# A third pass over token pairs in scaled float16 parts, with its second product in seven block products too

## The chip, the cores and the metric

The kernel runs on one core of a Trainium2 chip. The metric is device time in microseconds for one execution. A core has a matrix engine (TensorE, PE in the profile; its weight loads are listed as PEld), a vector engine (DVE), a scalar engine (ACT), GpSimd (POOL) and a queue that issues DMAs (SP). Matmuls read SBUF and write PSUM.

## The reference

Attention over 4 batches, 8 heads, 768 positions of 64, with a local window and block summaries, gives x, 3072 tokens of 512. Then a mixture of four experts works on x, with all experts on every token:

```python
def _moe_ref(x, domain_probs, w1, w2):            # x 3072 x 512, w1 4 x 512 x 1024, w2 4 x 1024 x 512
    p = domain_probs / (domain_probs.sum(-1, keepdims=True) + 1e-09)
    for e in range(E):
        h = np.maximum(x @ w1[e], 0.0)
        out += p[:, e:e + 1] * (h @ w2[e])
    ...

def reference(...):
    attn_out = _attn_ref(...)                     # softmax over a window of +-16 and 24 block summaries
    x = attn_out.transpose(0, 2, 1, 3).reshape(B * S, H * D)
    return _moe_ref(x, ...)
```

All data are float32.

## The kernel before

**Precision.** A float32 operand is split into a high part in fp32r (a rounded form of float32 that TensorE takes in one pass) and a low part, what the high part leaves. A product is three matmuls: high x high, high x low, low x high.

**Tokens and passes.** The 3072 tokens are eight blocks of 384 (`TB`). `plan` lists the passes of the experts over them: block 0 with experts 0 and 1, block 1 with 1 and 0, both with 2 and 3, and then `PAIRS`: pair 1 (blocks 2 and 3) with experts 3, 2, 1, 0, pair 2 (blocks 4, 5) with 0, 1, 2, 3 and pair 3 (blocks 6, 7) with 3, 2, 1, 0. Attention for later blocks runs between the matmuls of earlier passes, in 64 pieces (`load_piece`, `stage_a`, `scores`, `probs`, `transposed`, `values`, `to_x`); `advance` spreads their steps over the passes so that the last piece ends within pair 2's pass. Pair 3's pass has only the experts.

**A pair pass.** `pair_units` does one expert on one pair. The first product, x @ w1, uses seven block products in place of eight: the 2 x 2 blocks are two halves of the 512 rows of w1 and two blocks of 128 columns on one side, two token blocks on the other. For each of four groups i (two blocks of 128 columns of w1), the seven entries of `SEVEN` are six matmuls of 384 columns each, into four PSUM banks a, b, c, d: ACT copies a to b after entry 0 and d to SBUF (`five`) after entry 1, DVE makes c = b + five after entry 2 and d = b + five after entry 4. `to_h` then takes each finished bank: ACT writes relu as the high part, DVE the low part, straight from PSUM. The second product, h @ w2, is plain: `mm2` makes for each of the pair's six tiles of 128 tokens 24 matmuls of 512 columns (8 chunks, three matmuls each), and DVE adds the result, times the token's mixing weight, to `acc`; after the fourth expert the tile goes out by a DMA.

**Operands.** `x_operands` makes the seven sums of x for a pair, each split; `w1_operands` the seven sums of w1 for one group, `split_weights` the parts of w2. The first time (pair 1 for the sums of w1) raw weights are loaded, split by ACT, DVE and POOL, and the split parts are also stored to device memory (`stored`); later passes load the stored parts, 28 of 256 KB for w1 and 8 of 512 KB for w2 per expert. `fetch` runs one group ahead of the products, and `with_fetch` loads two groups during the second product.

**Order.** After the first tokens' part, order on each engine is set by the tile framework: it simulates a timeline with its own costs and issues by priority, which is the order of the code; `high_priority(offset=RUSH)` moves the PSUM copies, sums and relus ahead. Engines then run their queues in that order. Buffers come by tag with a fixed number each: x 14 (`NX`), w1 14 (`NW1`), w2 8, wr (raw weights) 4, hs 2, hh and hl 16 each, acc 6. Every engine call passes through one helper line (75), so the profile names groups by their tiles: `po` is the second product's PSUM, `pha` to `phd` the banks of a pair's first product, `psc` and `px` attention's, `w1s` and `w` parts of weights, `hh` and `hl` parts of h.

## Time and profile before

| | |
|---|---|
| median of 3 runs | 1188.52 us (1187.16 to 1191.98) |
| the profiled execution, time | 1190.1 us |
| its span, first to last instruction | 1188.3 us |
| mean granted TensorE clock | 0.994 |
| instructions | 19862 |
| DMA, q1 | 248.34 MB, 69.5% of 16 engines' span |
| HBM read / written | 174.22 / 57.15 MB |

Pair 1's pass runs from about 384 to 663 us after the span's start, pair 2's to 935, pair 3's to the end. In the views, a line of a group has the shapes, the count, the busy time in us, the mean length of one in ns, and the idle time before with what ended it. A line of the timeline or of the chain has the start and the time in us; with "x3", three instructions of that kind were merged, and the time reaches from the first one's start to the last one's end. An instruction's length reaches from its start to its written result; the next one on the engine may start before that.

### The profile page before, as it was taken

The page shows a single profiled execution, that of the slowest core. Times are in us where ns is not written, and L with a number is a line of the kernel's source. Part 1 is how long each engine was busy: PE and PEld are TensorE (multiplying, and loading weights), DVE is VectorE, ACT ScalarE, POOL GpSimd, SP SyncE. Part 2 cuts the span into 40 slices and gives each one's busy share as a digit, 9 for nine tenths or more (in the row PEclk, how much of TensorE's full clock was granted, in tenths as well). Part 3 has the DMA queues.
Part 4 walks back from the last instruction along what each step waited for, and adds up shares of the span by engine and source line. Part 5 has one row for each costly group of instructions (what it writes and reads, how often), then busy time and mean ns, then how long its engine had stood idle before and what let it go on. Part 6 is the DMA issues. An engine that isn't in the chain of part 4 may idle for free.

```text
span 1188.3 us, 19862 instructions
## 1 busy us (share of the span) xinstructions
PE 1155.9 (97%) x6740; PEld 1018.8 (86%) x6740; DVE 640.2 (54%) x1567; ACT 544.3 (46%) x1594; POOL 473.2 (40%) x586
## 2 busy tenths in 40 slices
PE   9898899999998999999999999999999999999998
PEld 7788778888977989888898988989898998989896
DVE  6668585554797756648587543535345322323131
ACT  5577567664665746547375443535333220202020
POOL 2388686855696746546384222222203000000000
PEclk9989999999999999999999999999999999999999
DMA  6699869975986879879973758769471556556421
GB/s 238 220 283 262 241 173 270 264 198 148 319 239 193 271 236 263 245 247 289 297 240 109 211 167 268 223 195 305 115 229 42 160 176 194 179 181 201 159 98 54
DMA packets 202709, 249.60 MB, mean 210 GB/s; under 512 B 83056, under 2 KB 118896, under 8 KB 202608
## 3 DMA queue, kind: packets, MB, share of 16 engines
q1 hardware_dynamic: 202608, 248.34, 69.5%
q8 instruction: 53, 0.87, 0.3%
q14 instruction: 48, 0.39, 0.1%
HBM read 174.22 MB, written 57.15 MB: 195 GB/s over the span
## 4 chain that ended last, share of the span: by engine, by line
PE 67%; DVE 5%; DMA 2%; POOL 1%; ACT 1%; issue 1%; SPq 0%; DVEq 0%; POOLq 0%; ACTq 0%
PE po L75 37%; PE phb L75 11%; PE pha L75 7%; PE phc L75 4%; PE phd L75 4%; PE psc L75 2%; PE px L75 2%; POOL wr L75 1%; DVE xr L75 1%; DVE w1s L75 1%; DMA wr<-in_w2L 1%; PE ph L75 1%; DVE xl_t L75 1%; DVE ms L75 0%; DVE hl L75 0%
## 5 line engine op out<-in xcount | busy, mean ns | idle before, releaser
L75 PE MATMUL po<-w,hh 128*128 128x512 f32 x1536 | 482.0, 395 | 1.8 <-DVE hl L75 1.8
L75 PEld LDWEIGHTS po<-w,hh 128*128 128x128 f32 x1536 | 284.8, 189 | 63.6 <-DVE hl L75 2.3
L75 PE MATMUL po<-w,hl 128*128 128x512 f32 x768 | 303.2, 397 | 0.2 <-DVE hl L75 0.2
L75 PEld LDWEIGHTS po<-w,hl 128*128 128x128 f32 x768 | 144.7, 188 | 31.9 <-DVE hl L75 0.6
L75 POOL TENSOR_TENSOR ks<-kr,ks 128x304 fp32r<-128x304 f32 x112 | 102.1, 919 | 93.0 <-ACT ks L75 82.5
L75 PE MATMUL phb<-xh_t,w1s 128*128 128x384 f32 x384 | 114.8, 339 | 1.7 <-DVE phc L75 0.8
L75 DVE CUSTOM_DVE_ANT_0 ms<-psc,c_sb 96x152 f32<-96x152 f32 x256 | 69.0, 306 | 85.1 <-PE psc L75 82.2
L75 ACT ACTIVATE ms<-ms,nb 96x152 f32<-96x152 f32 x256 | 104.3, 415 | 19.5 <-DVE nb L75 18.6
L75 PE MATMUL pha<-xh,w 128*128 128x384 f32 x384 | 110.6, 335 | 0.0
L75 DVE SCALAR_TENSOR_TENSOR acc<-po,pw,acc 128x512 f32<-128x512 f32 x72 | 52.2, 747 | 103.9 <-PE po L75 103.9
L75 POOL TENSOR_TENSOR qv<-qv,v 128x256 f32<-128x256 f32 x56 | 42.1, 753 | 161.3 <-ACT v L75 140.0
L75 PE MATMUL ph<-xh,wh 128*128 128x384 f32 x256 | 87.7, 349 | 12.8 <-ACT wh L75 5.3
L75 PE MATMUL ph<-xh,wl 128*128 128x384 f32 x256 | 87.0, 341 | 0.4 <-POOL wl L75 0.3
L75 PE MATMUL ph<-xl,wh 128*128 128x384 f32 x256 | 86.9, 340 | 0.0
L75 ACT CAST v<-qv 128x256 bf16<-128x256 f32 x112 | 44.7, 401 | 87.5 <-PE px L75 73.4
L75 ACT CAST aw<-ms 96x512 f16<-96x512 f32 x112 | 53.4, 524 | 68.2 <-issue 49.1
L75 POOL TENSOR_TENSOR wl<-wr,wh 128x512 fp32r<-128x512 f32 x44 | 60.8, 1386 | 53.2 <-ACT wh L75 50.2
L75 DVE TENSOR_TENSOR aw<-ms,aw 96x512 f16<-96x512 f32 x112 | 71.5, 671 | 16.7 <-ACT aw L75 16.6
L75 PEld LDWEIGHTS phb<-xh_t,w1s 128*128 128x128 f32 x384 | 70.8, 188 | 4.1 <-DVE phc L75 1.7
L75 PEld LDWEIGHTS pha<-xh,w 128*128 128x128 f32 x384 | 70.5, 188 | 0.4
L75 ACT CAST ks<-kr 128x304 fp32r<-128x304 f32 x112 | 48.2, 444 | 40.3 <-PE psc L75 38.0
L75 PE MATMUL phb<-xl_t,w1s 128*128 128x384 f32 x192 | 64.3, 335 | 0.0
(123 smaller groups left out, 2190.2 us busy)
## 6 DMA issues: line engine op xcount, KB each, us to landing
w<-wd SPq DMA_DIRECT2D x80, 512.0 KB, 4.4
w1s<-wds SPq DMA_DIRECT2D x112, 256.0 KB, 3.5
w<-wd SPq DMA_DIRECT2D x84, 256.0 KB, 3.4
wr<-in_w1L SPq DMA_DIRECT2D x76, 256.0 KB, 4.3
qv<-in_qvL SPq DMA_DIRECT2D x56, 320.0 KB, 3.9
wd<-w SPq DMA_DIRECT2D x32, 512.0 KB, 4.0
wds<-w1s SPq DMA_DIRECT2D x64, 256.0 KB, 2.4
kr<-in_kD SPq DMA_DIRECT2D x56, 256.0 KB, 3.7
```

The source lines that it names most:

```text
L75: ins = getattr(self.engine, name)(*a, **kw)
```

## The change

Pair 3's pass is rewritten; passes before it gain what it needs.

- **Scaling.** `SCALED` is pair 3. Maxima of |v| of the last batch (in `setup_v`), of |w1| and of |w2| for each expert (`scan`, called from `w1_operands` on the raw halves and from `pair_units` after entries 4 and 5 on w2's high part, each chunk once, so in pair 1's pass) give powers of two (`scales`) that bring operands near a fixed size; `over_partitions` takes a maximum over the 128 partitions by writing it to device memory and reading it back to all of them. x is multiplied by its scale in `x_operands`, weights as they are split, and `mixed` puts the inverse scales into the mixing weights.
- **float16.** High and low parts of x, w1, h and w2 in pair 3's pass are float16, in place of fp32r.
- **`seven_units`** takes the place of `pair_units` for pair 3. The first product has the same seven entries and six matmuls of 384 columns an entry. ACT now writes relu of each bank as float32 to SBUF, sums of h are made there (four DVE sums a group), and the seven operands of h are split by ACT copies and low parts (three on POOL, four on DVE). The second product uses the same seven entries: for each of three token tiles of the two blocks, seven entries of 12 matmuls with 256 columns, in banks a to d; `add_up` adds a finished bank to 256 columns of `acc`.
- **Weights** of pair 3's pass are not stored parts: `jobs_of` yields, an expert ahead, loads of raw weights and `make_group`, which splits one group of w1 or w2 (ACT casts with the scale, DVE low parts, POOL sums). A step of it is issued after each entry of the second product; those of the pass's first expert during pair 2's last second product. w1's groups take the tag w1; w2's take, for every other expert, the w2 tag or buffers that attention used (`ROOMS`).
- `fetch` covers pairs 1 and 2 only.

```diff
+    SCALED = NTB // 2 - 1
...
+    def over_partitions(m, k, name):
+        room = dram.tile([P, k], F32, name=f"{name}d")
+        SP.dma_start(room, m)
+        every = sb.tile([P, P, k], F32, name=f"{name}e", tag="hs", bufs=2)
+        flat = room.rearrange("p k -> (p k)").rearrange("(o n) -> o n", o=1)
+        SP.dma_start(every.rearrange("p q k -> p (q k)"), flat.broadcast_to([P, P * k]))
+        V.tensor_reduce(m, every.rearrange("p q k -> p k q"), axis=AX.X, op=ALU.max)
...
         def part(ib):
             ...
+            if pr == SCALED:
+                V.tensor_scalar(raw, raw, x_scale[pr][0], None, op0=ALU.mult)
...
+    def scan(e, which, fc, part):
+        ...
+        V.tensor_reduce(
+            t[:, which, fc : fc + 1], part, axis=AX.X, op=ALU.max, apply_absolute_value=True
+        )
+        if len(seen) == 2 * FC:
+            ...
+            over_partitions(m, 2, f"w{e}")
+            s, inv = scales(m, 2, f"w{e}")
...
+        scan(e, 0, 2 * pr, r1)          # in w1_operands, raw halves
+        scan(e, 0, 2 * pr + 1, r2)
...
+    def make_group(which, e, i):
+        s = w_scale[e][which]
+        r1, r2 = raws.pop((which, e, i))
+        ...
+        def parts(names, t, raw):
+            hi, lo = ...
+            A.activation(hi, raw, AF.Copy, scale=s)
+            V.scalar_tensor_tensor(lo, raw, s, hi, op0=ALU.mult, op1=ALU.subtract)
+            ...
+        if which == 0:
+            parts(("11", "12"), a, r1)
+            parts(("22",), d, r22)
+            PL.tensor_tensor(r22, r21, r22, op=ALU.add)
+            PL.tensor_tensor(r21, r11, r21, op=ALU.subtract)
+            parts(("s3", "s1"), b, r2)
+            PL.tensor_tensor(r11, r22, r11, op=ALU.subtract)
+            PL.tensor_tensor(r12, r12, r11, op=ALU.subtract)
+            parts(("s2", "s4"), c, r1)
+        else:
+            ...
+    def jobs_of(e):
+        steps = [(which, e, i) for which in range(2) for i in range(FC // 2)]
+        yield raw_group(*steps[0])
+        for here, after in zip(steps, steps[1:] + [None]):
+            if after:
+                yield raw_group(*after)
+            yield make_group(*here)
...
-    for pr, es in PAIRS:
+    for pr, es in PAIRS[:-1]:
...
+                if m in (4, 5):                                  # in pair_units
+                    fc = (f1, f2)[m - 4]
+                    scan(e, 1, fc, w2[fc][0].bitcast(F32))
...
+    def seven_units(pr, e):
+        ...
+        def split(w, i, src, lo):
+            tag = "hh" if w in ("11", "12", "22", "s1") else "hl"
+            t = sb.tile([P, 2, TB], F16, name=f"h{w}{e}_{i}", tag=tag, bufs=2 * FC)
+            A.copy(t[:, 0], src)
+            lo.tensor_tensor(t[:, 1], src, t[:, 0], op=ALU.subtract)
+            hs[w, i] = t[:, 0], t[:, 1]
+
+        def products(bank, new, operands, n, after):
+            for m, (k, a, b) in enumerate(SEVEN):
+                ...
+                for j, (l, r) in enumerate(todo):
+                    PE.matmul(bank[k], l, r, ...)
+                with rush():
+                    if m == 0:
+                        bank["b"] = new("b")
+                        A.copy(bank["b"], bank["a"])
+                    elif m == 1:
+                        five = sb.tile([P, TB], F32, ..., tag="hs", bufs=2)[...]
+                        A.copy(five, bank["d"])
+                    elif m == 2:
+                        bank["c"] = new("c")
+                        V.tensor_tensor(bank["c"], bank["b"], five, op=ALU.add)
+                    elif m == 4:
+                        V.tensor_tensor(bank["d"], bank["b"], five, op=ALU.add)
+                after(m)
+                yield 6 * US1, SLOW
+        for i in range(FC // 2):
+            ...
+            def after(m):
+                if m < 3:
+                    return
+                src, r = {3: ("a", r11), 4: ("d", r22), 5: ("c", r21), 6: ("b", r12)}[m]
+                with rush():
+                    A.activation(r, bank[src], AF.Relu)
+                if m == 3:
+                    split("11", i, r11, PL)
+                elif m == 4:
+                    split("22", i, r22, PL)
+                elif m == 5:
+                    V.tensor_tensor(r22, r21, r22, op=ALU.add)
+                    split("s1", i, r22, V)
+                    V.tensor_tensor(r21, r11, r21, op=ALU.subtract)
+                    V.tensor_tensor(r11, r22, r11, op=ALU.subtract)
+                    split("s2", i, r11, V)
+                    split("s3", i, r21, V)
+                else:
+                    split("12", i, r12, PL)
+                    V.tensor_tensor(r12, r12, r11, op=ALU.subtract)
+                    split("s4", i, r12, V)
+        ...
+        jobs = jobs_of(PAIRS[-1][1][following]) if following < E else iter(())
+        for t in range(TB // P):
+            ...
+            def after(m):
+                if m >= 3:
+                    k = "adcb"[m - 3]
+                    add_up(tbs[k in "bd"] * (TB // P) + t, e, bank[k], 256 * (k in "cd"))
+                next(jobs, None)
+            yield from products(bank, new, operands, f"2{e}_{t}", after)
```

More of the change, by code (lines that the diff above doesn't have):

```diff
@@ L45 @@
 NW1 = 14
+TOP = 2.0
+LEAST, MOST = 2.0**-100, 2.0**100
 ASC = 32768.0
@@ L363, in split @@
             A.copy(hi, raw)
-            lo.tensor_tensor(low, raw, hi.bitcast(F32), op=ALU.subtract)
+            lo.tensor_tensor(low, raw, hi if pr == SCALED else hi.bitcast(F32), op=ALU.subtract)
         def part(ib):
@@ L692, in split_early @@
         split[0, fc, which] = split_weights(loaded.pop((0, fc, which)), 0, fc, which, *a)
+    tops = {}
+    def scan(e, which, fc, part):
+        if e not in tops:
+            tops[e] = const.tile([P, 2, FC], F32, name=f"wt{e}"), []
+        t, seen = tops[e]
+        if (which, fc) in seen:
+            return
+        seen.append((which, fc))
+        V.tensor_reduce(
+            t[:, which, fc : fc + 1], part, axis=AX.X, op=ALU.max, apply_absolute_value=True
+        )
+        if len(seen) == 2 * FC:
+            m = const.tile([P, 2], F32, name=f"wm{e}")
+            V.tensor_reduce(m, t, axis=AX.X, op=ALU.max)
+            over_partitions(m, 2, f"w{e}")
+            s, inv = scales(m, 2, f"w{e}")
+            both = const.tile([P, 1], F32, name=f"wi{e}")
+            V.tensor_tensor(both, inv[:, 0:1], inv[:, 1:2], op=ALU.mult)
+            w_scale[e] = s[:, 0:1], s[:, 1:2], both
     WS = ("11", "s2", "s1", "s3", "12", "s4", "22")
@@ new lines, in jobs_of, with mixed @@
+    def jobs_of(e):
[5 more added lines that the diff above has]
+            yield make_group(*here)
+    mix = {}
+    def mixed(pr, e):
+        gts = range(2 * pr * (TB // P), 2 * (pr + 1) * (TB // P))
+        if pr not in mix:
+            mix[pr] = sb.tile([P, len(gts), E], F32, name=f"pm{pr}", tag="pm")
+            for k, gt in enumerate(gts):
+                mix["t", gt] = mix[pr][:, k]
+        V.tensor_scalar(
+            mix[pr][:, :, e : e + 1], pw[:, gts[0] : gts[-1] + 1, e : e + 1], x_scale[pr][1], w_scale[e][2],
+            op0=ALU.mult, op1=ALU.mult,
+        )
@@ L789, in fetch, with second @@
                 return
-    def second(tbs, e, hT, w2, last):
-        whole = tbs if last else tbs[:-1]
+    def second(tbs, e, hT, w2):
+        whole = tbs[:-1]
         for tb in whole:
@@ L847, in attn_moe, with pair_units @@
     )
-    def pair_units(pr, e, last=False):
+    def pair_units(pr, e):
         tbs = (2 * pr, 2 * pr + 1)
@@ L955, in attn_moe @@
         for e in experts:
-            if pair:
-                units = pair_units(pair, e, last=nxt == NTB // 2 and e == experts[-1])
+            if pair == SCALED:
+                units = seven_units(pair, e)
+            elif pair:
+                units = pair_units(pair, e)
             else:
                 units, ahead = ahead or plain_units(tbs, e, last=n == 2 and e == experts[-1]), None
+            first_job = jobs_of(PAIRS[-1][1][0]) if pair == SCALED - 1 and e == experts[-1] else iter(())
             for us, pace in units:
@@ L969, in attn_moe @@
                         parts.pop(0)()
+                    next(first_job, None)
+            for _ in first_job:
+                pass
         advance(end)
```

139 lines of the change are left out of this document (126 added, 13 removed).

## The prediction

> **What bounds the kernel now.** I read the page's busy times and slices first, then the windows by stage, then the chain of work that ended last, then single lengths.
>
> ```profile
> PE 1155.9 (97%) x6740; PEld 1018.8 (86%) x6740; DVE 640.2 (54%) x1567; ACT 544.3 (46%) x1594; POOL 473.2 (40%) x586
> DVE  6668585554797756648587543535345322323131
> ACT  5577567664665746547375443535333220202020
> POOL 2388686855696746546384222222203000000000
> ```
>
> ```profile
> 384.00:663.00 279.00, 277.31 (x1617) 243.76 (x1616) 183.51 (x434) 152.20 (x466) 157.53 (x204) 1.00 0.78 238
> 663.00:935.00 272.00, 272.00 (x1571) 240.31 (x1570) 125.46 (x320) 107.53 (x313) 56.63 (x80) 1.00 0.65 192
> 935.00:1188.30 253.30, 249.57 (x1248) 224.27 (x1246) 68.73 (x121) 43.68 (x96) 0.00 (x0) 1.00 0.51 161
> ```
>
> The columns are the stretch, its length, then busy time of PE, weight loads, DVE, ACT and POOL, the granted clock and the DMA share. The three rows are the three pair passes. In the third, TensorE is busy from its start to 3.7 us before the end at clock 1.00, DVE 27%, ACT 17% and POOL not at all. So the pass lasts as long as its matmuls, and the three other engines have room. The chain shows the pitch of the matmuls:
>
> ```profile
> 1012.89 2.08 PE phb L75 x12
> 1033.38 28.42 PE po L75 x123
> ```
>
> A 384-column product takes 2.08/12 = 0.173 us, a 512-column one 28.42/123 = 0.231 us: 0.451 ns a column in both. An expert has 4 x 42 of the first and 6 x 24 of the second: 29.1 + 33.3 = 62.4 us, four experts 249.5 us, which is the window's 249.57.
>
> **The change on TensorE.** First products keep their 672 matmuls of 384 columns; the second ones become 4 x 3 x 7 x 12 = 1008 of 256 columns in place of 576 of 512; the operands become float16. No row has a float16 matmul with 128 weight columns, the nearest is the bfloat16 one that keeps the array warm at the start:
>
> ```profile
> 7.77 1.47 PE L75 MATMUL pz<-z 128*128 128x512 bf16 x7
> L75 PE MATMUL pz<-z 128*128 128x384 bf16 x4 | 0.8, 326 | 0.0
> 656.33 0.49 PE L75 MATMUL psc<-ks,qs 128*96 128x152 f32 x4
> 503.50 0.57 PE L75 MATMUL psc<-ks,qs 128*96 128x152 f32 x4
> ```
>
> The first seven are three of 512 and four of 384 columns, each with weights of its own. The last lasts 0.326, so the first six took 1.47 - 0.33 = 1.14 us for 2688 columns: 0.425 ns a column, not 0.451. That makes 0.163 us for 384 and 0.109 us for 256. Per expert 168 x 0.163 + 252 x 0.109 = 27.4 + 27.5 = 54.9 us, four 219.6: **29.9 us less**, if TensorE stays the bound. The unknown is whether a weight load hides under 256 columns. Lower end: nothing on top of the columns. Upper end: the score products, 152 columns on fresh weights of four bytes each; the four lie (0.49 - 0.25)/3 = 0.08 and (0.57 - 0.25)/3 = 0.107 us apart where columns alone make 0.065 (0.25 is how long one lasts), so up to +0.04 a matmul, +42 us. I take 0.109, since the warm row is the nearer one: 128 two-byte weight columns, fresh each time, and none of it seen.
>
> **The change on the other engines.** In pass three each group of h (four an expert) now has four ReLUs, seven copies and two PSUM copies on ACT, seven low parts (four DVE, three POOL) and four sums of h plus two PSUM sums on DVE. The weights are no longer read back split, but raw, and split here for the next expert: eight groups, each four ACT casts, four DVE low parts and four POOL sums. Lengths:
>
> ```profile
> L75 DVE SCALAR_TENSOR_TENSOR acc<-po,pw,acc 128x512 f32<-128x512 f32 x72 | 52.2, 747 | 103.9 <-PE po L75 103.9
> L75 DVE SCALAR_TENSOR_TENSOR hl<-pha,hh 128x384 fp32r<-128x384 f32 x48 | 26.3, 549 | 10.6 <-ACT hh L75 10.6
> L75 DVE TENSOR_TENSOR aw<-ms,aw 96x512 f16<-96x512 f32 x1 | 0.7, 689 | 0.3 <-ACT aw L75 0.3
> L75 ACT CAST qs<-qv 128x384 fp32r<-128x384 f32 x56 | 28.6, 511 | 3.7 <-PE psc L75 3.4 <-POOL xl L75 0.3
> L75 ACT CAST wh<-wr 128x512 fp32r<-128x512 f32 x44 | 27.2, 617 | 16.9 <-DMA wr<-in_w1L 16.1 <-PE ph L75 0.2
> L75 POOL TENSOR_TENSOR ks<-kr,ks 128x304 fp32r<-128x304 f32 x112 | 102.1, 919 | 93.0 <-ACT ks L75 82.5 <-DMA w<-wd 8.6 <-DMA qv<-in_qvL 1.2
> L75 POOL TENSOR_TENSOR wr<-wr 128x256 f32<-128x256 f32 x32 | 26.2, 819 | 10.9 <-DVE w L75 10.0
> 919.85 0.60 POOL L75 TENSOR_TENSOR xl_t<-xr,xh_t 128x192 fp32r<-128x192 f32 x1 [0.68 <-ACT xh_t L75]
> wr<-in_w1L SPq DMA_DIRECT2D x76, 256.0 KB, 4.3
> 920.86 1.40 DVE L75 SCALAR_TENSOR_TENSOR acc<-po,pw,acc 128x512 f32<-128x512 f32 x2
> 914.19 0.86 ACT L75 CAST xh<-xr 128x192 fp32r<-128x192 f32 x3 [2.96 <-DMA xr<-xd]
> ```
>
> Back to back an instruction costs less than it lasts: two sums into acc fill 1.40 us, so the second adds 0.65, about 0.08 under its length; three casts of 0.35 fill 0.86, 0.255 each, 0.095 under. ACT per expert: 52 x 0.41 for h, 6 x 0.31, and 8 x (3 x 0.52 + 0.31) for weights: 38 us of 55. POOL: 12 x 1.05 + 32 x 0.75 = 36.6 us. Both fit.
>
> DVE is where it gets tight. What reads PSUM: 8 x 0.47 + 6 x 0.34 + 12 x 0.40 (256 columns, from 0.67 less 256 elements at 1.04 ns) = 10.6 us. What reads two tensors in SBUF: 32 x 0.47 for h and 8 x (3 x 0.66 + 0.40) for weights = 34.0 us. Alone that is 44.6 of 54.9. But POOL works beside it now, and these rows of pass two's end show what that does:
>
> ```profile
> 915.26 2.77 DVE L75 TENSOR_TENSOR xr<-xr 128x192 f32<-128x192 f32 x4 [3.44 <-POOL xl L75]
> 922.18 0.35 DVE L75 TENSOR_TENSOR xr<-xr 128x192 f32<-128x192 f32 x1
> 914.62 3.88 POOL L75 TENSOR_TENSOR xl<-xr,xh 128x192 fp32r<-128x192 f32 x6 [7.67 <-ACT xh L75]
> L75 DVE TENSOR_TENSOR aw<-ms,aw 96x512 f16<-96x512 f32 x1 | 1.2, 1200 | 0.0
> ```
>
> The same DVE sum lasts 0.35 alone and 0.69 while POOL runs; the last row, from 595 to 605 us, is the 0.689 us instruction of the fence before (from 868 to 890 us, hardly any POOL) at 1.2. With POOL busy for 37 of some 59 us (63%) and DVE at about half speed then on its SBUF pairs, the 34.0 become 34.0 / (1 - 0.63 x 0.47) = 48.3, and with 10.6 that is **58.9 us** an expert: more than TensorE's 54.9. I add 2 us for queues in order (a cast that waits for POOL holds the PSUM copy behind it on ACT, a low part that waits for the cast holds the PSUM sums on DVE, and TensorE waits for both): **61 us** for the three experts that split weights for the next. The fourth splits none: 54.9 plus 1.5 at the joint between its products = 56.5. Pass three: 3 x 61 + 56.5 = 239.5 in place of 249.5: **-10 us**. Ends: -28 if DVE keeps up, +13 if a cycle takes 68.
>
> A weight group holds two of the four raw buffers until its last part: a load of 4.3 us, then seven engine steps in a row, some 8 us; two groups at a time make 6 us a group, 48 us for eight. That is covered by the 61. If queueing doubles the steps, it is 10 us a group, 80 us, and w2 comes late; this is in the upper end.
>
> **Elsewhere.** The scans: 32 reductions over raw w1 and 32 over w2's high part, all in pass one.
>
> ```profile
> L75 DVE TENSOR_REDUCE vsr<-vch 128x24 f32<-128x768 f32 x12 | 11.4, 948 | 17.7 <-DMA vch<-in_vT 17.7
> 454.00:486.00 32.00, 31.15 (x205) 29.93 (x204) 25.31 (x56) 22.26 (x68) 23.19 (x30) 1.00 1.01 279
> 594.00:625.00 31.00, 30.23 (x200) 28.41 (x199) 26.36 (x62) 21.49 (x66) 25.33 (x30) 1.00 0.78 240
> 902.00:935.00 33.00, 33.00 (x149) 27.45 (x148) 13.60 (x30) 7.33 (x23) 6.32 (x10) 1.00 0.14 48
> ```
>
> 948 ns for 768 elements make 0.68 for 512, 0.60 back to back: 38 us more for DVE, some 7 of them in each expert's first products, where DVE is already busy 25 to 26 of 31 us and TensorE loses 0.8. The second products of pass one have half of DVE free, which covers the rest. POOL's sums overwrite the raw blocks, so they now wait for the scan, and ACT's and DVE's parts behind them; the one group of lead (42 x 0.173 = 7.3 us) covers 1.2 us. I take **+3**, between 0 and +12 (half a microsecond a group to all that does not fit). The maxima over partitions are ten small DMAs on SP's queue, two in a row each of five times; the second waits for the first, and loads behind it on SP wait too, some 4 us, under the same lead; 0, at worst +5, in the same bounds. The scale on x, four DVE instructions, and the three-operand weights of the mixture are under 3 us on DVE, in the last row's stretch.
>
> That stretch must also split the first expert's weights: DVE 13.6 + 4 + 8 x 2.4 alone, about 42 beside POOL, in 33 us. The w1 half comes first and fits; the w2 half has the 27 us of the first products. **+1**, from 0 to +5. The tail stays: one 256-column sum and the same output DMA. DMA work falls, as 28 split parts of 256 KB and 8 of 512 KB an expert become 16 raw ones of 256 KB; the queue did not bound the pass, so 0.
>
> Sum: -10 + 3 + 1 = -6 against the profiled execution's 1190.1, hence 1184.1. That one lies 1.6 over the median of the three runs, so **1182.5**. About 0.5% (6 us) is what can be told from no change.
>
> **A rule that speaks against it.** The Trainium skill, SBUF — State Buffer, section Who interferes with whom, says that a DVE instruction with two SBUF inputs and a GpSimd instruction that reads SBUF exclude each other by a lock, while one with a single SBUF input is free. The second half agrees with the rows below: a low part read from PSUM takes 545 ns in pass one, beside POOL, and 551 in pass three, without. On the first half the 2.77 us stretch is milder: four DVE sums of 0.27 and 4.3 of POOL's would need some 3.5 us one after the other.
>
> ```profile
> L75 DVE SCALAR_TENSOR_TENSOR hl<-pha,hh 128x384 fp32r<-128x384 f32 x15 | 8.2, 545 | 1.5 <-ACT hh L75 1.5
> L75 DVE SCALAR_TENSOR_TENSOR hl<-pha,hh 128x384 fp32r<-128x384 f32 x15 | 8.3, 551 | 3.9 <-ACT hh L75 3.9
> ```
>
> **Rivals.**
> - *TensorE-paced* (chance 0.21). The 47% loss applies only where both overlap; if the order on the queues keeps POOL's work off DVE's, the cycle is 55 to 57. In favour: pass one runs DVE at 80% with TensorE at 98%. Then -29.9 + 3 x 1 + 4 for the joints + 3 + 1 = -19, 1170; down to 1164 without joints and scans.
> - *Slower: DVE and POOL exclude each other* (0.22). 34.0 and POOL's 36.6 less a tenth (0.60 alone in the fence of lengths, 3.88/6 = 0.65 beside DVE), so 33.5, one after the other are 67.5 an expert, the second products wait for their low parts: 3 x 68 + 57 = 261, +11.5, with +4 elsewhere 1204. It turns into a loss from a cycle of 63 us on. In favour: the 1.2 us row; against: the 2.77 us one. By the rule above, taken strictly, it is this rival.
> - *The scans eat it* (0.08). Pass one pays 12 or more, 1192 to 1196.
> - *256 columns don't hide the weight load* (0.05). +0.04 each is 65 us an expert, above DVE's 59; 4 x 65 = 260, +10.5, with +4 elsewhere 1203, and about 1190 for half of it.
>
> **How the numbers follow.** My own case has 0.44, its range 1174 to 1192 (cycle 58 to 64). Of it some 0.25 lie below 1182.6, 0.16 within 0.5%, 0.03 above. With the rivals: faster 0.25 + 0.21 + 0.01 = 0.47; same 0.16 + 0.03 (exclusion) + 0.05 (scans) + 0.02 (weights) = 0.26; slower 0.03 + 0.19 + 0.02 + 0.03 = 0.27. The range leaves a tenth on each side: 1164 to 1206.
>
> **What would show it.** Right: matmuls of pass three at 0.163 and 0.109 us; DVE over 90% busy in its first three experts, TensorE with gaps released by DVE and ACT; SBUF-pair instructions of DVE at 0.7 to 1.1 us; POOL near 63%; about 61 us between experts and 56 for the last; pass one longer by a few microseconds. Wrong: TensorE at 97% or more there (too pessimistic), cycles over 63 us, gaps released by weight loads, or a pass one that is 10 us longer.

## The result and the profile after

The changed kernel takes 1243.8 us (median of 4 runs, 1240.33 to 1246.33), the kernel before 1187.84 (4 runs, 1186.27 to 1191.98): 1.0463 times as long, interval 1.0426 to 1.0501. The forecast was 1182.5, with a range that ended at 1206. The profiled execution took 1243.0 us; its span is 1241.2. From the page of after, the busy times and three rows of the 40 slices:

```profile
PE 1162.1 (94%) x7172; PEld 974.3 (78%) x7172; DVE 849.4 (68%) x1922; ACT 675.6 (54%) x1858; POOL 641.4 (52%) x762
...
PE   9898999999989998999899999999989869698798
...
DVE  6676675656997757577785535444488896968854
...
PEclk9998899999989999999899999999999979899899
```

TensorE, at 97% before, is at 94%, although its work shrank. In the last quarter its row and the clock row have dips that before had not, and DVE's row, 1 to 5 there before, stands mostly at 8 and 9. The windows give the passes (first three rows; each begins with the pass's first matmul) and pass three's four experts (a row from one expert's first matmul to the next one's). The columns are those of the prediction's windows.

```profile
385.20:677.50 292.30, 282.19 (x1613) 247.43 (x1612) 211.62 (x527) 152.82 (x466) 155.52 (x204) 0.98 0.78 233
677.50:958.30 280.80, 276.57 (x1572) 241.50 (x1571) 152.96 (x353) 126.55 (x345) 86.70 (x112) 0.99 0.67 199
958.30:1241.20 282.90, 238.11 (x1678) 167.67 (x1677) 216.55 (x332) 154.51 (x328) 140.10 (x144) 0.93 0.17 52
958.30:1028.60 70.30, 56.05 (x383) 38.51 (x382) 62.50 (x89) 43.46 (x90) 43.68 (x44) 0.90 0.25 75
1028.60:1103.90 75.30, 62.67 (x422) 43.03 (x420) 60.59 (x91) 43.08 (x90) 42.42 (x44) 0.89 0.21 60
1103.90:1178.00 74.10, 60.09 (x422) 41.67 (x421) 59.80 (x90) 43.11 (x90) 42.75 (x44) 0.93 0.15 43
1178.00:1241.20 63.20, 59.30 (x458) 44.47 (x456) 33.66 (x63) 24.86 (x58) 11.26 (x12) 1.00 0.07 26
```

By first matmuls the kernel before has 278.2, 271.8 and 253.6 us. So the 52.9 us by which the span grew are +14.1 in pass one, +9.0 in pass two, +29.3 in pass three (and 0.5 ahead of them). An expert's first matmuls are issued among the last second products of the expert before, of which 36 (3.9 us) follow. So the first row lacks 3.9 us, and the last has 3.9 us too many and another 3.4 after its last matmul: 63.2 is 56 for one expert alone, which is TensorE's own time.

The matmuls got their price. From TensorE's timeline, then from the chain that ended last:

```profile
1190.75 1.14 PE L78 MATMUL phb<-x_t,g_0d 128*128 128x384 f16 x6
```

```profile
1223.34 2.62 PE pob L78 x24
```

The length of one is 0.326 here, so the first is (1.14 - 0.33)/5 = 0.163 us for 384 columns, the second 2.62/24 = 0.109 for 256. No time goes to weight loads.

What failed is seen in one cycle, the third, cut into nine slices:

```profile
1103.90:1112.10 8.20, 8.20 (x65) 6.09 (x64) 2.76 (x6) 2.38 (x5) 0.00 (x0) 1.00 0.00 0
1112.10:1120.40 8.30, 8.30 (x53) 5.00 (x52) 4.70 (x8) 4.65 (x12) 6.54 (x8) 1.00 0.00 0
1120.40:1128.60 8.20, 7.27 (x45) 4.28 (x44) 8.06 (x14) 7.19 (x16) 3.86 (x4) 1.00 0.23 66
1128.60:1136.90 8.30, 8.30 (x57) 5.29 (x54) 5.69 (x10) 7.30 (x18) 5.48 (x7) 1.00 0.25 63
1136.90:1145.10 8.20, 3.51 (x19) 1.95 (x19) 8.20 (x9) 4.11 (x10) 7.45 (x8) 0.89 0.11 32
1145.10:1153.30 8.20, 5.86 (x41) 3.93 (x39) 8.20 (x12) 6.05 (x14) 5.60 (x6) 0.90 0.25 66
1153.30:1161.60 8.30, 2.26 (x9) 0.87 (x10) 8.30 (x12) 4.42 (x10) 4.24 (x5) 0.72 0.19 57
1161.60:1169.80 8.20, 8.20 (x68) 6.90 (x66) 7.85 (x15) 4.04 (x7) 6.17 (x7) 0.87 0.34 104
1169.80:1178.10 8.30, 8.30 (x78) 7.44 (x77) 6.04 (x11) 2.98 (x6) 3.41 (x4) 1.00 0.01 2
```

In the middle, 24.7 us around the joint between the two products, DVE is busy without a pause (8.20 of 8.20 and so on) and TensorE works 11.6 of them. In the first two slices DVE works 7.5 of 16.5. Over the whole cycle that averages to 59.8 of 74.1, which looks like room. TensorE's timeline at the joint shows what it waits for there, at the end of each row:

```profile
1142.27 0.39 PE L78 MATMUL pod<-g_2b,hs 128*128 128x256 f16 x2 [3.73 <-ACT hs L78]
...
1154.02 0.28 PE L78 MATMUL poa<-g_3a,h 128*128 128x256 f16 x1 [1.40 <-POOL h L78]
1155.57 0.39 PE L78 MATMUL pod<-g_3b,hs 128*128 128x256 f16 x2 [1.26 <-DVE hs L78]
1157.11 0.61 PE L78 MATMUL pob<-g_3c,hs 128*128 128x256 f16 x2 [1.15 <-ACT hs L78]
1160.16 0.40 PE L78 MATMUL pob<-g_3c,hs 128*128 128x256 f16 x1 [2.44 <-DVE hs L78]
```

All are parts of h, of its last groups. In front of them and between them, on DVE and POOL, the tile framework has put parts and sums of the next expert's weights, w1 first (`g_2b<-wr,w0s`, `wr<-wr`). They hold h up twice. Of DVE's 24.7 us, ten parts of weights take 8.0; h's own 18 sums and parts take 15.3, which at 0.47 each, without POOL beside them, would be 8.5. DVE's and POOL's timelines between 1137 and 1142:

```profile
1138.61 1.07 DVE L78 TENSOR_TENSOR hs<-hr_1b,hs 128x384 f16<-128x384 f32 x1
1139.60 1.07 DVE L78 TENSOR_TENSOR hs<-hr_1a,hs 128x384 f16<-128x384 f32 x1
1140.60 1.07 DVE L78 TENSOR_TENSOR hr_2b<-hr_2b 128x384 f32<-128x384 f32 x1
1141.59 1.21 DVE L78 SCALAR_TENSOR_TENSOR g_2b<-wr,w0s,g_2b 128x512 f16<-128x512 f32 x1
```

```profile
1138.23 1.03 POOL L78 TENSOR_TENSOR wr<-wr,wr 128x256 f32<-128x256 f32 x1
1139.23 2.03 POOL L78 TENSOR_TENSOR wr<-wr 128x256 f32<-128x256 f32 x2
1141.21 1.03 POOL L78 TENSOR_TENSOR wr<-wr,wr 128x256 f32<-128x256 f32 x1
```

From 1138.6 to 1141.6 DVE gets through three instructions and POOL through three, one each a microsecond; alone they follow each other at 0.47 and 0.69. They nearly take turns, some 15% faster than one after the other.

In pass one the place is DVE's queue again (DVE's timeline, with the idle time before and its releaser at the end):

```profile
472.72 0.69 DVE L78 TENSOR_REDUCE wt<-wr 128x1 f32<-128x512 f32 x1 [2.74 <-DMA wr<-in_w1L]
473.33 0.56 DVE L78 TENSOR_TENSOR phc<-phb,p 128x384 f32<-128x384 f32 x1
...
609.42 0.69 DVE L78 TENSOR_REDUCE wt<-w 128x1 f32<-128x512 f32 x1 [5.26 <-DMA w<-wd]
610.02 0.68 DVE L78 TENSOR_TENSOR v<-v,b 120x512 f32<-120x512 f32 x1
610.62 0.30 DVE L78 CUSTOM_DVE_ANT_0 ms<-psc,c_sb 96x152 f32<-96x152 f32 x1
```

A scan that waits for its load holds the PSUM sum or the attention maximum behind it, and TensorE waits for those: its two longest gaps of the pass, 3.4 us at 470 and 3.6 us at 608. In all TensorE is idle for 10.1 us of pass one (292.30 - 282.19), where before had 1.7 (279.00 - 277.31): 8.4 of the 14.1 us. The rest is busy time that grew, and 10.2 us behind the two gaps run at half clock, which makes 5.1.

### The profile page after: what moved, and what is told of

It reads as the page before. It is cut to its first block, busy times and chain, and to the rows that moved or that the text cites. A ratio compares the mean times of both kernels' runs of the same rounds, so it can differ in the third digit from the quotient of the medians.

```text
span 1241.2 us, 21547 instructions
## 1 busy us (share of the span) xinstructions
PE 1162.1 (94%) x7172; PEld 974.3 (78%) x7172; DVE 849.4 (68%) x1922; ACT 675.6 (54%) x1858; POOL 641.4 (52%) x762
## 4 chain that ended last, share of the span: by engine, by line
PE 65%; DVE 15%; DMA 10%; issue 4%; ACT 3%; POOL 2%; SPq 1%; DVEq 0%; POOLq 0%; ACTq 0%
PE po L78 26%; PE phb L78 9%; PE ph L78 6%; PE pha L78 5%; PE pob L78 4%; PE psc L78 4%; PE phc L78 3%; PE phd L78 2%; PE px L78 2%; DMA w<-wd 2%; DVE hs L78 2%; DMA wr<-in_w2L 2%; PE poa L78 1%; PE poc L78 1%; DMA kch<-in_kT 1%
## 5 line engine op out<-in xcount | busy, mean ns | idle before, releaser
L78 PE MATMUL po<-w,hh 128*128 128x512 f32 x1152 | 365.5, 399 | 2.1 <-DVE hl L78 1.8
L78 PEld LDWEIGHTS po<-w,hh 128*128 128x128 f32 x1152 | 214.7, 191 | 49.4 <-DVE hl L78 3.1
L78 PE MATMUL po<-w,hl 128*128 128x512 f32 x576 | 228.5, 401 | 0.5 <-DVE hl L78 0.5
L78 PEld LDWEIGHTS po<-w,hl 128*128 128x128 f32 x576 | 109.5, 190 | 25.3 <-DVE hl L78 1.3
L78 POOL TENSOR_TENSOR wr<-wr 128x256 f32<-128x256 f32 x96 | 85.8, 898 | 68.4 <-DVE g_0d L78 33.7
L78 POOL TENSOR_TENSOR wr<-wr,wr 128x256 f32<-128x256 f32 x96 | 86.2, 900 | 33.8 <-DVE g_1a L78 13.2
L78 PEld LDWEIGHTS <-hs 128*128 128x128 f16 x576 | 57.5, 102 | 40.4 <-ACT hs L78 12.9
L78 ACT CAST v<-qv 128x256 bf16<-128x256 f32 x112 | 44.7, 401 | 75.2 <-PE px L78 62.5
L78 PE MATMUL phb<-xh_t,w1s 128*128 128x384 f32 x256 | 78.5, 347 | 4.8 <-DVE phc L78 3.4
L78 PE MATMUL pha<-xh,w 128*128 128x384 f32 x256 | 74.4, 336 | 0.0
L78 PE MATMUL psc<-ks,qs 128*96 128x152 f32 x448 | 60.0, 255 | 5.6 <-DVE nb L78 4.2
```

The source lines that it names most:

```text
L78: ins = getattr(self.engine, name)(*a, **kw)
```

## The experiments

Medians in us, and the lengths of the passes in each kernel's profiled execution. The ratio is to the kernel before on the same chip (1187.5 to 1190.3). Each version ran two to eight times.

| run | median | ratio, interval | pass 1 | pass 2 | pass 3 |
|---|---|---|---|---|---|
| before | 1187.8 | | 278.2 | 271.8 | 253.6 |
| after | 1243.8 | 1.0463, 1.0426 to 1.0501 | 292.3 | 280.8 | 282.9 |
| e1_rush_h | 1243.8 | 1.0450, 1.0416 to 1.0485 | 293.1 | 280.2 | 286.3 |
| e2_no_scan | 1235.0 | 1.0379, 1.0348 to 1.0410 | 278.2 | 280.3 | 281.5 |
| e3_no_split | 1186.9 | 0.9966, 0.9939 to 0.9993 | 293.1 | 283.7 | 227.2 |
| e4_warm | 1247.7 | 1.0471, 1.0436 to 1.0506 | 289.3 | 280.2 | 287.8 |
| e5_side_sums | 1265.1 | 1.0646, 1.0597 to 1.0695 | 290.7 | 286.8 | 302.2 |
| e6_dve_sums | 1220.9 | 1.0274, 1.0158 to 1.0389 | 291.7 | 278.3 | 271.5 |
| e7_no_sums | 1230.6 | 1.0356, 1.0311 to 1.0400 | 293.1 | 281.3 | 270.5 |
| e8_late_scan | 1236.2 | 1.0402, 1.0353 to 1.0452 | 290.9 | 280.8 | 282.7 |
| e9_gate | 1234.0 | 1.0389, 1.0337 to 1.0440 | 293.6 | 280.5 | 274.9 |
| e10_gate_early | 1218.2 | 1.0255, 1.0192 to 1.0318 | 289.9 | 280.1 | 263.1 |
| e11_gate_dve | 1215.1 | 1.0229, 1.0177 to 1.0281 | 290.7 | 276.9 | 261.8 |
| e12_scan_two | 1239.4 | 1.0434, 1.0330 to 1.0539 | 280.9 | 290.9 | 283.7 |
| e13_scan_gate | 1233.6 | 1.0386, 1.0365 to 1.0407 | 285.9 | 278.9 | 283.1 |
| e14_stash | 1247.5 | 1.0503, 1.0482 to 1.0524 | 297.8 | 303.0 | 263.6 |
| e15_stash_all_gate | 1216.6 | 1.0234, 1.0214 to 1.0253 | 290.1 | 287.5 | 254.9 |
| e16_half_w1 | 1230.9 | 1.0363, 1.0333 to 1.0393 | 292.4 | 281.8 | 272.4 |
| e17_half_w2 | 1210.8 | 1.0194, 1.0162 to 1.0226 | 289.7 | 283.2 | 252.6 |
| e18_stash_w1 | 1212.1 | 1.0181, 1.0152 to 1.0211 | 289.2 | 291.2 | 250.5 |

Twelve of these kernels have the same code in pass one, and it takes them 289.3 to 293.6 us: that much is scatter. The profiled executions of e6, e12 and e18 lie 5, 5 and 8 us over their kernel's median, those of e2 and e4 4 and 6 us under it, so passes and median differ by as much.

**First round: which part of the change pays.**

e1: h's copies, sums and low parts issued with raised priority.

```diff
-            A.copy(t[:, 0], src)
-            lo.tensor_tensor(t[:, 1], src, t[:, 0], op=ALU.subtract)
+            with rush():
+                A.copy(t[:, 0], src)
+                lo.tensor_tensor(t[:, 1], src, t[:, 0], op=ALU.subtract)
```

> The change with h's copies, sums and low parts in pass three put at the same raised priority as the PSUM copies; no instruction is added or taken away. Theory 1, order of the queues: h's parts of the last two groups wait on DVE, ACT and POOL behind weight parts that only the next expert needs, so the joints between first and second product stall; with h ahead the cycle of an expert falls from 75 to 60 to 62 us, and the time from 1243.8 to about 1203. Theory 2, throughput: DVE and POOL hinder each other on SBUF and DVE has no more time to give; the order changes little, cycles stay at 70 or more, 1233 to 1245. Theory 3, the clock: gaps halve TensorE's clock; it would follow the gaps, so this run alone does not tell it from theory 1.

No gain, and the order on DVE in pass three differs from the changed kernel's by two instructions that moved one place, of 331. My reading, which no run shows, is that the planner (the tile framework's simulated timeline, which orders the queues) already had h's parts early in its own reckoning and fills with weights what it takes for free time. So this priority hardly moves the order, and the run says nothing on what another order would do.

e2: constant scales, no maxima.

```diff
-        if e not in tops:
-            ...
+        if e not in w_scale:
+            w_scale[e] = fixed(32.0, f"ws{e}"), fixed(32.0, f"wt{e}"), fixed(2.0**-10, f"wi{e}")
```

> The change without the maxima: no scans of w1, w2 and v, no exchange over the partitions; the scales are constants (8 for x, 32 for w1 and w2) that these inputs allow. Theory A, the scans on DVE delay pass one: its 292 us fall back to 278, the total to about 1229, pass three as before. Theory B, the 14 us come from elsewhere (another order of the same work, w1's and w2's loads): pass one stays within 4 us of 292, the total at 1240 or more.

Pass one is at 278.2 us, what it was before, so all its 14 us belong to the maxima and their exchange. Passes two and three hardly move. The median gains 9 and not 14: the profiled execution, itself 4 us under the median, reached pass one 4 us later, and where those arise was not followed.

e3: the last three experts load the first one's split parts (24 of 32 weight groups not split; the values differ).

```diff
+        if e != PAIRS[-1][1][0]:
+            for t, k in zip((a, b, c, d), saved[which, i]):
+                SP.dma_start(t, k)
+            ...
+            return
```

> The change where the weights of the last three experts of pass three are not split: their groups are loaded as parts that the first expert's jobs have stored, so the weights of these three are those of the first. 24 of 32 groups of ACT casts, DVE low parts and POOL sums go, the parts of h stay. If the weight splitting is what the pass pays: cycles of 75 us become 52 to 55, the time about 1180. If h's own parts in seven sums are too much for DVE and ACT: cycles stay at 65 or more, 1210 or more. If the first expert's cycle, which makes its parts earlier, stays at 70: it is the parts left from pass two.

Windows of pass three and of its third expert:

```profile
960.20:1187.40 227.20, 220.08 (x1670) 162.60 (x1669) 128.89 (x236) 98.55 (x231) 44.85 (x48) 1.00 0.33 108
1068.50:1124.20 55.70, 55.25 (x423) 40.99 (x421) 31.49 (x58) 24.85 (x58) 10.91 (x12) 1.00 0.42 133
```

Without the splitting the pass is TensorE's: 55.25 of 55.7 us at clock 1.00, where I had worked out 54.9. So h's own sums and parts fit behind the matmuls, and splitting the weights beside them costs 56 us of pass three.

e4: 40 further matmuls of 256 columns per expert at the head of the second products, to keep TensorE from idling.

```diff
+                    if n == f"2{e}_0" and m < 2 and j in (6, 9):
+                        for _ in range(10):
+                            PE.matmul(full[k][:, 256:512], xp["11"][0][:, 0, 0:P], ..., stop=False)
```

> The change with 40 more matmuls an expert (256 columns, into unread columns of the same banks) in the first token tile of the second product, before the third and fourth group of entries 0 and 1, where TensorE waits for h: 4.4 us of matmuls an expert at full clock. Theory 3, the clock: the gaps are filled, the half clock of 41 us in pass three is mostly gone, and the time falls by 12 to 18 us, to about 1228. Theories 1 and 2: TensorE waits for the same parts as long, so the time stays within 4 us of 1243.8; where the added matmuls run without a gap to fill, they cost up to 4 x 4.4 = 18 us.

In pass three, time at half clock falls from 41 to 31 us, the pass doesn't get shorter. What the lower clock costs by itself stays open, since the fillers take time too.

**Second round: POOL beside DVE, or the chain cast, sum, cast, low part.**

e5: POOL's sums are computed into a buffer that nobody reads. e6: they move to DVE. e7: they are left out (in e5 and e7 raw blocks stand for the sums). e8: the scans are issued later.

```diff
-            PL.tensor_tensor(r22, r21, r22, op=ALU.add)          # and the seven others
+            PL.tensor_tensor(spare_sum, r21, r22, op=ALU.add)    # e5
+            V.tensor_tensor(r22, r21, r22, op=ALU.add)           # e6; e7 has no line here
```

> POOL's four sums per weight group are still computed from the raw blocks at the same place, but into a buffer that nobody reads, and ACT's casts and DVE's low parts take the raw blocks (so the weights are not the sums). POOL's reads and writes of SBUF beside DVE stay; the chain cast, sum, cast, low part is cut. Theory A (DVE and POOL slow each other in SBUF): DVE's pair instructions stay at 0.7 to 1.25 us, the cycles stay near 75 us, total 1235 to 1245. Theory B (the chain across three engines in queues that run in order is what stalls; contention is already in DVE's 60 us): cycles fall to 61 to 64 us, total 1200 to 1210.

> POOL's sums of the weights are made by DVE instead: 32 more DVE instructions an expert (0.33 to 0.47 us each, 11 to 15 us), POOL keeps only three low parts a group of h. Contention goes, the chain stays but has one engine less. Theory A: DVE's pairs fall to their lengths alone (0.55 for 384, 0.74 for 512), DVE is 57 to 60 us busy an expert with hardly a wait, cycles 62 to 64, total 1205 to 1212. Theory B: DVE and ACT still wait for each other, cycles stay at 70 to 75, total 1225 to 1245. A third theory, that DVE's own load sets the time, gives the same or longer cycles, 75 to 80.

> POOL's sums of the weights are left out (the parts are split from raw blocks, so the result differs): neither contention nor the chain over POOL. Both theories A and B: DVE busy near 46 us, cycles 55 to 58 us, pass three 225 to 235 us, total 1187 to 1195, as where the weights were not split at all. If cycles stay over 62, neither POOL's contention nor its sums are the cause, but the casts and low parts on ACT and DVE in the way of h's parts.

One expert's cycle in e5, then in e7:

```profile
1119.00:1198.60 79.60, 62.63 (x423) 42.75 (x421) 62.45 (x90) 42.68 (x90) 37.24 (x36) 0.87 0.14 40
```

```profile
1095.30:1166.20 70.90, 61.34 (x422) 43.17 (x420) 51.96 (x90) 42.04 (x90) 13.31 (x12) 0.90 0.15 45
```

The chain is not what stalls: cut in e5, the pass is 19 us longer. Why it is longer was not followed. Contention is real: e5 and e7 differ only in POOL's sums, and DVE's busy time falls from 62.5 to 52.0 us, the pass by 32. But it isn't the whole cause: with most of it gone and DVE at 52 of 70.9 us, the cycle is still 15 us over TensorE's. Both of my theories gave 55 to 58 there; what held is the third reading put down with them, that casts and low parts of weights are in the way of h's parts. Three slices of e7's cycle show the same joint:

```profile
1126.90:1134.80 7.90, 4.83 (x36) 3.31 (x35) 7.90 (x14) 7.77 (x17) 2.35 (x2) 1.00 0.25 66
1134.80:1142.70 7.90, 5.03 (x23) 3.26 (x23) 7.90 (x14) 6.08 (x13) 1.54 (x2) 0.59 0.43 137
1142.70:1150.60 7.90, 4.27 (x23) 2.53 (x21) 7.90 (x15) 5.04 (x11) 0.83 (x1) 0.72 0.09 33
```

For 23.7 us DVE has no pause and TensorE works 14.1, with POOL hardly busy. e6 gains 11 us of pass three, less than its theory A gave.

e8's edit moves `scan` behind the first two splits of a group (w1) and into the second products (w2).

> Same maxima, issued later: those of w1's raw halves after the first two splits of the group (ahead of POOL's sums that overwrite them), those of w2's parts in the second products, long after their load has landed. Theory W (what the scans cost is that DVE's queue stands while a scan waits for its DMA, w<-wd 20.3 us and wr<-in_w1L 12.9 us in pass one): pass one falls from 292 to 280 to 284 us and the total to 1231 to 1236. Theory L (it is the scans' own 38 us of DVE time): pass one stays at 290 to 293, total 1240 to 1246.

Pass one stays at 290.9. But DVE waits for the same loads as long (20.7 us for w2's against 20.3): it seems that the planner puts the scans where it believes the data to be there, whatever the place in the code. The waits did not move, so the run decides nothing on them; of its median's 8 us, 4 lie ahead of pass one.

**Third round: the place in the queue.** In the changed kernel the planner pulls the next expert's w1 splits forward into the first products, as soon as buffers are free. e9 forbids that with a dependence: the scale by which weights are multiplied passes through an instruction that reads the last sum of h.

```diff
+            V.scalar_tensor_tensor(
+                gated[nxt_e], last["r"][:, 0:2], 0.0, w_scale[nxt_e][3], op0=ALU.mult, op1=ALU.add
+            )
```

> The scale with which an expert's weights are split is passed through one small DVE instruction that reads the last sum of h of the expert before it, so no cast or low part of weights can be issued in the first products of the expert before; all eight groups come behind them, in the second products and the next first products. Theory J (weight parts that were pulled forward stand in front of the last parts of h; DVE is 100% busy for 24 us around the joint and idle for most of 16 us at the cycle's end): the gaps at the joint go, h's DVE pairs fall back to 0.55 us, the cycles become 58 to 63 us, total 1200 to 1212. Theory C (DVE, POOL and ACT cannot do this work in under 75 us however it is placed): w2's parts come late instead, the wait moves to the head of the next second product, cycles 72 to 80, total 1238 to 1255.

> The same, but the small instruction reads the last sum of the third of the four groups of h, some 7 us earlier. Theory J: part of the weights stands in front of the fourth group's parts again, cycles between the gated ones and 75 us, 62 to 68, total 1210 to 1225. Theory C: the more time for the weights the better, cycles below those of the later gate.

> The gate of the last h sum, and POOL's sums of the weights on DVE as well. DVE then needs about 57 us an expert with nearly no contention. Theory J: cycles 60 to 64 us, total 1203 to 1215, no better than the gate alone, because 32 sums of 0.35 to 0.45 us cost DVE as much as the contention did. Theory C: chain and contention both shortened, cycles shorter than with the gate alone by 5 us or more.

```profile
957.90:1014.40 56.50, 52.83 (x383) 37.84 (x383) 38.88 (x70) 31.50 (x70) 20.13 (x23) 0.97 0.13 41
```

e9's first expert needs 56.5 us in place of 70.3: with no weights in front, TensorE idles for 3.7 us of it in place of 14.3. The second needs 68.1, the third 74.7: all eight groups now come behind the joint, and the wait moved to the next first products. The earlier gate, which J expected to be worse and C better, is better by 12 us of pass three, and the late gate with POOL's sums on DVE by 13. So J has the joint right and C the rest; neither gave e9's total. ACT's timeline of e11 shows the new wait:

```profile
1087.31 0.71 ACT L78 ACTIVATE g_2b<-wr,wg 128x512 f16<-128x512 f32 x1
1089.94 0.72 ACT L78 ACTIVATE g_2c<-wr,wg 128x512 f16<-128x512 f32 x1 [1.93 <-DVE wr L78]
...
1093.61 0.72 ACT L78 ACTIVATE g_3c<-wr,wg 128x512 f16<-128x512 f32 x1 [1.72 <-DVE wr L78]
1094.23 0.47 ACT L78 ACTIVATE hr_0a<-pha 128x384 f32<-128x384 f32 x1
```

Casts of w2, each late for a load or a sum, stand in front of the ReLU of h's first group, and TensorE waits 8.1 us for that ReLU's bank. It seems that the planner counted on the casts being earlier.

e12: three experts' maxima in pass two, where DVE was 54% busy; w1's are taken from four of its seven split sums.

```diff
+                if m >= 3 and pr == 2 and e != PAIRS[-1][1][0]:
+                    scan(e, 0, 4 * i + m - 3, ready[pr, e, i][("11", "12", "22", "s3")[m - 3]][:, 0:256].bitcast(F32))
```

> Maxima of three of the four experts' weights are taken in pass two instead of pass one: w2 from its high part as before, w1 from the high parts of four of its seven sums (a bound within a factor of two, so the scales may be half as large). Both theories on the scans (waits for DMA in DVE's queue, or their 38 us of DVE time in a pass where DVE is 80% busy) let pass one fall from 292 to 278 to 281 us. In pass two DVE is busy 46%: by its load alone nothing is added, 281 stays and the total is 1230 to 1234; if the waits for loaded parts stall DVE's queue there as well, pass two grows by 3 to 8 us and the total is 1234 to 1242.

```profile
667.60:958.50 290.90, 281.32 (x1578) 244.05 (x1576) 175.94 (x437) 124.75 (x345) 85.54 (x112) 0.98 0.67 194
```

Pass one gains 11 us, pass two loses 10 with DVE at 176 of 291 us. Over the pass its load leaves room, which speaks against the scans' own time as the reason, if only by the average. DVE waits 26.3 us there for w2's loads with a scan in hand.

**Fourth round.** e13: all maxima in pass one again (w1's from split sums, as in e12), each behind an instruction that reads a late result, so that a scan can't reach the head of the queue before its data.

```diff
+        V.tensor_scalar_mul(col, late, 0.0)
+        V.tensor_reduce(col, part, axis=AX.X, op=ALU.max, apply_absolute_value=True)
```

> All maxima stay in pass one, but each is tied to a result that comes late: a small DVE instruction writes the maximum's column from a low part of h first (w1 from four of its seven high parts, in the group's own products; w2 one group after its load was issued), so a scan cannot stand in DVE's queue before its data have landed. DVE's work is the same or a little more. Theory W (the queue stands behind late data): pass one 279 to 284 us in place of 292, total 1231 to 1237. Theory L (the scans' 38 us of DVE time): 290 to 294, total 1241 to 1247.

```profile
382.30:668.20 285.90, 280.88 (x1613) 246.15 (x1612) 223.25 (x669) 153.37 (x463) 155.31 (x204) 0.98 0.78 238
```

DVE works more than in the changed kernel (223 against 212 us), and the pass is 6.4 us shorter. The gap at 470 and the half clock behind it are gone, so W holds for that part. The rest sits at one spot: around 586 to 602 DVE waits 4.95 and 1.91 us for maxima read back from device memory (`w1e<-w1d`, `ve<-vd`), and TensorE has its longest gap, 3.4 us, and 10 us at half clock. e15 and e18 below have the same scans; the gap at 470 is gone there too, but the one at the read-back is longer and pass one takes 290.1 and 289.2, the lower end of its scatter. So what the tied scans are worth stays open, up to 6 us.

e14: three experts' weights split in pass two and stored, loaded in pass three. e15: all four experts' (and e13's scans).

```diff
+                if pr == SCALED - 1 and m in (0, 4) and later:
+                    stash(*later.pop(0))       # loads, casts, sums, low parts, four stores
```

> The weights of pass three's last three experts are split during pass two, with the same casts, low parts and sums, and stored as float16 parts; pass three loads them. In pass two DVE was busy 153 of 281 us, ACT 127, POOL 87; this adds some 57, 60 and 72. Theory P (place: the work harms where it shares queues with h's parts that TensorE waits for next): pass three 224 to 230 us as where the weights weren't split, pass two +2 to +8, total 1190 to 1200. Theory A (amount, or late chains in any queue): pass two grows by 15 to 40 us, and total stays over 1205.

> Both: the maxima tied as in the first of these runs, and all four experts' weights split during pass two. By theories W and P: pass one 281, pass two 275 to 285 (nothing to split at its end, but more before), pass three 224 to 230, total 1172 to 1190, at least level with the kernel before. If W fails 10 us more, if P fails 1205 or more.

Experts whose weights were ready in time need 55.6 to 58.3 us in both, as in e3. But the work did not fit into pass two. In e14 the last of the twenty-four groups is split at 978, so the first expert's own splits begin at 981, with pass three: TensorE waits 16 us for them and 24 for a ReLU that stands behind them. In e15 the last of the thirty-two is split at 1099, and two cycles are still 65 and 71 us. DMA engines are at 90 and 97% in pass two; whether they limit it or the four raw buffers was not tested. P holds for the experts that were ready, not for pass three as a whole (263.6 and 254.9, where it gave 224 to 230) and not for the total.

e16 and e17 halve the work: of the last three experts only w1's groups are split, or only w2's (the others are the first expert's, loaded).

```diff
+        if e != PAIRS[-1][1][0] and which == 1:    # e16; which == 0 in e17
+            for t, k in zip((a, b, c, d), saved[which, i]):
+                SP.dma_start(t, k)
```

> For the last three experts only w1's groups are split; w2's are the first expert's parts, loaded (so the values differ). DVE needs about 46 us an expert instead of 60. Theory Q (the planner pulls w1's groups forward into the first products of the expert before, where they stand in front of h's parts): gaps at the joint stay, cycles 62 to 68 us, total 1205 to 1225. Theory A (amount alone): half the loss of 20 us goes, cycles 65, total 1215. Theory K (a threshold: with 46 of 55 us DVE has slack): cycles 56 to 59, total 1187 to 1197.

> The other half: only w2's groups are split, w1's are loaded. Theory Q: w2's groups are split in the second products, where DVE is free, so hardly a gap at the joint: cycles 56 to 59, total 1187 to 1197, shorter than with w1's groups by 5 us a cycle or more. Theory A: cycles 65, total 1215, the same as with w1's. Theory K: 56 to 59, the same as with w1's.

A cycle of e16 and its joint, then a cycle of e17:

```profile
1095.10:1165.60 70.50, 62.46 (x423) 42.89 (x421) 46.57 (x74) 33.16 (x74) 27.91 (x28) 0.90 0.35 120
...
1130.30:1139.20 8.90, 5.86 (x24) 3.46 (x25) 8.90 (x11) 6.15 (x13) 6.62 (x7) 0.62 0.14 50
1139.20:1148.00 8.80, 5.62 (x37) 3.11 (x35) 8.80 (x16) 4.07 (x11) 3.17 (x3) 0.88 0.31 116
```

```profile
1077.50:1144.90 67.40, 60.16 (x446) 43.83 (x445) 47.69 (x75) 34.06 (x75) 28.57 (x28) 0.97 0.37 126
```

The same number of instructions of the same kinds: with w1's half the cycles are 69 to 71 us and the pass 272.4, with w2's 59, 63 and 67 and 252.6. Place decides 20 us. In e16 DVE is busy 66% of the cycle and without a pause for 17.7 us at the joint. Theories A and K give the same for both halves and fall. Q has the order of the two right, but its ranges were too good for both (62 to 68 and 56 to 59). In e17's third cycle TensorE waits 5.7 us in the first products for PSUM sums (`phc`, `phd`): w2's parts of the next expert, pulled forward, stand in front of them on DVE.

e18: w1's twelve groups in pass two, w2's in pass three, e13's scans; the whole computation.

> w1's groups of the last three experts are split in pass two, stored and loaded in pass three; w2's groups are split in pass three; the maxima are tied to late results as before. By theory Q: cycles as with w2's half alone, 59 to 67 us, pass three about 253 us, pass two 281 to 288, pass one 286, total 1200 to 1212: 30 to 40 us under the changed kernel, still over the kernel before. If the amount decided, and not the place, the total would stay over 1225, since pass two would pay what pass three saves.

```profile
968.00:1218.50 250.50, 227.46 (x1672) 164.50 (x1671) 168.20 (x284) 125.95 (x279) 95.09 (x97) 0.96 0.26 78
```

Pass three is at 250.5, as Q gave; pass two pays 10, pass one is at 289.2 where 286 was expected. The median is 32 us under the changed kernel and the lowest of the versions with the whole computation, but 1.8% over the kernel before. None of them beats it.

## Why the prediction was wrong

Against the profiled execution the sum is 58.9 us short (1243.0 against 1184.1): 39 of it in pass three, 11 in the scans, 8 at the end of pass two.

- **Right.** 0.163 and 0.109 us a matmul; weight loads hidden; 54.9 us an expert of TensorE (55.25 in e3); the last expert 56.5 (56); DVE 58.9 us an expert (60.6 and 59.8); POOL 42.4 of 75 us (56%, where I had 63). DVE's figure is right term by term. In the second and third cycle its 64 SBUF pairs take 48.8 and 48.2 us; at the lengths that they have in the same trace without POOL (0.47 us from start to start for 384 columns, 0.66 and 0.40 for 512 and 256) they would take 34.5. That leaves 14.2 and 13.7 for contention, where I had 34.0 and 14.3, and 11.5 for what reads PSUM, where I had 10.6. In e7 it is 52 and not 44.6, because POOL's low parts of h still add 5.0.
- **The step that failed** is "I add 2 us for queues in order ... 61 us". Measured are 75.3 and 74.1, that is 14 to 15 over DVE's busy time. The step compares DVE's total with the cycle, as if it could be filled evenly. What the runs show is a deadline: h's last parts are due at the joint, and the planner had put the next expert's w1 parts in front of them, and POOL's sums beside them. DVE is full for 24.7 us there and half idle at the cycle's start; by the code, the 14 w1 buffers then still hold the current expert's four groups. TensorE loses 14.0 us idle in the third cycle (74.1 - 60.09) and 5.2 at half clock (60.09 - 54.9). e3, e7, e9's first expert and e16 against e17 show it from four sides. The bracket behind the 2 us names a neighbour of it: there PSUM copies and sums stand behind parts of weights, here h's own parts do, and they are due at one point. The sign that I had given for it came: cycles over 63 us. (A slip in the same step: the upper end "+13 if a cycle takes 68" is +11 by its own sum, 3 x 68 + 56.5 against 249.5.)
- **Contention as the bound.** The rival in which DVE and POOL exclude each other gave a cycle of 67.5 to 68 and 1204. In the fence of turns they nearly do: a pair of instructions takes 0.99 us, against 1.16 one after the other. The Trainium skill (SBUF — State Buffer, Who interferes with whom) has them exclude each other by a lock; the trace agrees there to 15%. But the cycles measured are 75, not 68, and taking POOL's sums away (e7) leaves 71. The rival had the sign right and the cause at most in part.
- **The scans**, +3 (0 to 12) for 14.1. I priced their busy time and the exchange's DMAs, not a scan's wait for its own data at the head of DVE's queue (20.3 and 12.5 us in pass one by the waits). Most of these waits cost TensorE nothing; two of them made the gaps of 3.4 and 3.6 us, and with half of the 10.2 us at half clock behind them that is 12 of the 14. In e13 the first of the two is gone. The second sign that I had given, a pass one that is 10 us longer, came too.
- **The transition**, +1 (0 to 5) for 9.0. I had 42 us of DVE work in 33 and let the rest run under the next matmuls. In the trace a PSUM sum (`phd`) sits behind x's and weights' parts on DVE, TensorE waits 3.1 us at 926 and then has 6.8 us at half clock, worth 3.4. No run took this part alone; that it is the same mechanism is argued only.
- **The clock.** I took 1.00 throughout. The granted clock fell to 0.5 in nine stretches from pass one on, 3.4, 6.8 or 10.2 us long, each at gaps of TensorE. In pass three they make 41 us: TensorE is busy there for 238.1 us in place of the 219.6 that I had worked out, and idle for 44.8. The Trainium skill (TensorE: Matmul & The Clock Gate, Part 1: The HAM clock gate) states windows of 3.4 us and a half rate after an idle one; the lengths agree, but the 3.4 us ahead of a stretch were not wholly idle: in this trace TensorE idled for 1.8 to 3.2 of them, several times in gaps of 1.2 to 1.4 us with short bursts between.

## What to carry to other kernels

A busy share over a cycle doesn't bound the cycle: cut the cycle into slices, mark where each result is due, and add up what stands in the queue ahead of that point. Work moved from DMA to the engines is only as free as its place; work for later that a planner pulls forward lands in front of work that is due now, and here a raised priority did not change that (e1), while a dependence did (e9). Price an instruction that reads freshly loaded data by its wait at the head of its queue and by who stands behind it, not by its length.

## What the runs showed of the hardware

- DVE (384 columns) and POOL (256 columns), both with two operands in SBUF, nearly take turns: 0.99 us for one of each, where alone 0.47 and 0.69 pass. Over an expert's cycle POOL added 14 us to DVE's 46.
- A gap of some 3.5 us can cost TensorE a second time: at 470 the gap is 3.4 us, and 3.4 us at clock 0.5 follow; in pass three 41 of 283 us ran at half clock. Before, pass one to three had none.
- float16 matmuls with 128 new weight columns each run at 0.425 ns a column down to 256 columns, the fp32r ones of the kernel before at 0.451.
